# A fp32 transformer block on one core: a chunk's starting sum copied into its PSUM bank during the chunk ahead of it, second-level weights prepared in every second step, four PSUM banks for the projection's last block

## The chip, the core and the metric

The kernel runs on one core of a Trainium2 chip. The metric is the device time of one execution in microseconds (us), read as the median of several runs. TensorE (PE) multiplies, VectorE (DVE), ScalarE (ACT) and GpSimd (POOL) prepare and evacuate, and SyncE (SP) issues every DMA of the kernel in one in-order queue. Each of these engines takes its instructions in the order in which they stand in the program.

## The reference, cut to what matters

```python
def _B_ref(x, w_gate, w_up, w_down):
    return (_gelu(x @ w_gate) * (x @ w_up)) @ w_down
...
h = _layernorm(x, axis=-1) * (1 + ca) + sa
x = x + ga * _A_ref(h, A_wq, A_wk, A_wv, A_wo, A_beta)
h = _layernorm(x, axis=-1) * (1 + cb) + sb
x = x + gb * _B_ref(h, B_w_gate, B_w_up, B_w_down)
```

There are 2048 tokens of width 1024. `_A_ref` is an attention with 32 heads over four segments of 512 tokens, with a running memory from segment to segment, and ends in the output projection `wo`. `_B_ref` is a gated feed-forward block with 3584 hidden columns. All data are fp32; the six rows `sa, ca, ga, sb, cb, gb` come from a small product of `c` and `w_mod`.

## The kernel before

The work on PE is one long list of matmuls, written in the order of the program: opening (modulation and first projections), attention, output projection, feed-forward. An fp32 operand is cut in two parts, a high one (an ACT copy) and a low one (a subtraction on DVE or POOL), and each product is three matmuls: high by high, high by low, low by high. The helper for this is `cut` (ACT line 926, DVE or POOL line 923); in the traces its output carries the name of the tile.

The feed-forward block saves matmuls by forming sums of quarter matrices: `seven` builds seven left operands out of four weight quarters (lines 1079 to 1099), `five` builds five (1101 on). Its stages, in the order in which PE runs them:

- **Projection** (`project`, line 753; called by `block` in `projections`). For each segment and column half it walks over four groups of 128 tokens. A group is 24 matmuls into one bank from `mm_ps`, which has two banks; DVE then adds the bank to a tile of `x` (line 777). The last block is segment 3, half 1. Beside it run generators which prepare the first operands of the next stage (`b_two(0)`, `a_early`, `a_first`).
- **Pairs** (`two`, line 1121), 14 of them. A pair n multiplies seven weight tiles `BB` with seven activation tiles `AA`, for two sets i of activation tiles, in the order r = 1, 5, 6, 2, 7, 3, 4, with i = 1 and then i = 2 for each r (the first pair has all of i = 1 first). A product is six matmuls. They land in the banks `pa`, `pb`, `pc`; `pb` starts from an ACT copy of `pa`, and `ended` evacuates a bank after each product (ACT lines 1156, 1158, 1164; DVE lines 1160, 1162, 1166). The results go to DRAM as `st_d`, one half of them through a gelu (line 1175). The weights of pair n + 1 are built meanwhile by `b_two(n + 1)`. The tiles `BB` live in eight buffers, so each new one takes the buffer of a tile of pair n, and has to wait until PE has used it.
- **Beside the pairs**, from pair 1 on, the generator `norm_tiles(..., "c", wait=6)` normalises the last segment. For each 128 tokens it has PE transpose two halves (`turn`, line 269, banks `tpc` from `o_ps`, which has a single bank); the first half is read by ACT (line 277) and the second by DVE (line 275). The branch of `norm_steps` for `wait` sets how many steps lie between the two (lines 293 to 310). `a_mix(0)` follows it.
- **Chunks** (`gate_up`, line 1359), 56 of them: 28 over the first half of the tokens, and 28 over the second in reverse order. A chunk loads two tiles `cg` from `st_d` (`cg_load`), the sum c1 from which it starts and the gelu g1. It takes two of the five banks `s_ps`: `pb`, into which ACT copies c1 (line 1386), and `pc`. Then come five products of twelve matmuls, in the order 6, 5, 7, 3, 4: 6, 7 and 4 into `pb`, 5 and 3 into `pc`, with evacuations behind each (ACT 1388, 1391; DVE 1394, 1397, 1398) and a last gelu out of `pb` (ACT 1401). In the trace both banks are named `f`.
- **Beside the chunks**, in the first half `b_part(m + 1)` builds the five weight tiles `B` of the next chunk and stores them (`bc_d`, `bt_d`) for the second half, where `b_ahead` and `b_again` load them again seven and six products ahead of their use; a tile `ag`, which `b_again` loads, is cut four products after the load is issued. `a_mix(1)` runs beside chunks 1 to 9. In the second half `w_all` builds the sums of the down weights (POOL multiplies `rw` and forms differences, ACT and DVE cut them as `T`, SP stores them as `wc_d`).
- **Down** (`down`), the last product, with tiles `y`.

What is written beside the matmuls is set by `step()` (line 799): each call sends the stores that are due and advances every generator in the list `sides` by the number of yields that stands with it. A pair calls `step()` after each of its 14 products; a chunk calls it twice in each product, ten times in all. `flush` runs the rest of a generator at once. So the order on ACT, DVE, POOL and SP is the order in which these calls emit.

## Time and profile before

| | us |
|---|---|
| median of 3 runs | 2819.65 (2818.3 to 2819.79) |
| the profiled execution, its own time | 2816.52 |
| its span, first to last instruction | 2814.8 |
| around the span | 1.72 |
| opening and attention end, projection begins | about 910 |
| first pair begins | 1119.72 |
| first chunk begins | 1430.88 |
| down begins | 2277 |

The profile gives for each engine the busy time; a matmul's record is longer than its share of the pipeline, so a busy PE overlaps itself. A row of the timeline has the start, the length, the engine, the line, the operation with its tiles and the count, and in brackets the idle time of the engine ahead of it with what ended it. A row of the windows has, for each engine, the busy time and the number of instructions, then the granted TensorE clock (1.00 is full), the mean busy share of the core's 16 DMA engines and the bytes they moved in GB/s.

### The profile page before, as it was taken

What the parts mean: (1) busy time and instruction counts of PE and PEld (TensorE: products, weight loads), DVE (VectorE), ACT (ScalarE), POOL (GpSimd) and SP (SyncE); (2) the same over time, 40 slices, a digit from 0 to 9 for tenths busy, and PEclk for the clock granted to TensorE, in tenths of its full rate; (3) what the DMA queues carried; (4) which work ended last, traced back from release to release, by engine and by line L of the source; (5) the groups of instructions that cost most, each with busy time, mean ns of one, the idle gap of its engine ahead of it and who ended that gap; (6) DMA issues with size and microseconds to landing.
All of it is one profiled execution on the core that took longest, in us unless ns stands there. A gap on an engine that the chain in (4) does not pass through costs nothing.

```text
span 2814.8 us, 42379 instructions
## 1 busy us (share of the span) xinstructions
PE 2691.4 (96%) x14073; PEld 2218.8 (79%) x14073; DVE 1652.6 (59%) x3540; ACT 1384.8 (49%) x3162; POOL 1013.9 (36%) x1554
## 2 busy tenths in 40 slices
PE   7999999999999999999989999999999999999999
PEld 6888888888888787777767777777777788888887
DVE  7677567667767456655565443454554545475456
ACT  6787777776677443655543333343333333233323
POOL 3333334434335431434357766644655400000000
PEclk9999999999999999999999999999999999999999
DMA  7455445444454485556689777789999887786554
GB/s 254 123 159 139 125 126 164 124 125 128 117 147 135 161 291 176 179 167 226 236 288 318 263 243 251 237 289 343 331 335 342 322 292 250 260 308 221 172 201 133
DMA packets 265644, 612.32 MB, mean 218 GB/s; under 512 B 26960, under 2 KB 51536, under 8 KB 265424
## 3 DMA queue, kind: packets, MB, share of 16 engines
q1 hardware_dynamic: 265424, 609.61, 65.1%
q8 instruction: 111, 1.82, 0.3%
q14 instruction: 109, 0.89, 0.1%
HBM read 371.48 MB, written 187.70 MB: 199 GB/s over the span
## 4 chain that ended last, share of the span: by engine, by line
PE 83%; DMA 5%; DVE 5%; ACT 4%; issue 2%; SPq 1%; POOL 1%; ACTq 0%; DVEq 0%; POOLq 0%
PE f L1375 24%; PE y L1575 18%; PE kv L395 9%; PE q L401 6%; PE y L773 4%; PE S L607 3%; PE O L707 3%; PE T L695 3%; PE pb L1139 3%; PE pc L1139 2%; PE pa L1139 2%; PE vT L514 1%; ACT f L1386 1%; PE kT L514 1%; DMA B<-bc_d 1%
## 5 line engine op out<-in xcount | busy, mean ns | idle before, releaser
L1375 PE MATMUL f<-A,B 128*128 128x512 f32 x3360 | 781.0, 392 | 70.7 <-ACT f L1386 70.7
L1375 PEld LDWEIGHTS f<-A,B 128*128 128x128 f32 x3360 | 627.7, 188 | 223.7 <-ACT f L1386 94.4
L1575 PE MATMUL y<-B,L 128*128 128x512 f32 x2352 | 533.6, 389 | 0.2 <-DVE L L923 0.2
L1575 PEld LDWEIGHTS y<-B,L 128*128 128x128 f32 x2352 | 441.4, 188 | 92.3 <-DVE L L923 0.6
L611 ACT ACTIVATE sj<-sj,mm 128x384 f32<-128x384 f32 (+3 forms) x512 | 281.1, 552 | 40.1 <-DVE mm L609 39.6
L698 POOL TENSOR_SCALAR_AFFINE_SELECT pt<-pt 128x128 f32<-128x128 f32 x512 | 166.6, 347 | 330.9 <-ACT pt L697 322.8
L609 DVE CUSTOM_DVE_ANT_0 sj<-S,mask 128x384 f32<-128x384 f32 (+3 forms) x512 | 228.2, 488 | 97.7 <-PE S L607 70.8
L697 ACT ACTIVATE pt<-T 128x256 f32<-128x256 f32 (+3 forms) x512 | 182.3, 444 | 132.3 <-PE T L695 125.4
L926 ACT ACTIVATE L<-X 128x512 fp32r<-128x512 f32 x168 | 105.7, 629 | 256.3 <-PE y L1575 164.7
L923 DVE TENSOR_TENSOR L<-X,L 128x512 fp32r<-128x512 f32 x168 | 115.8, 690 | 144.9 <-ACT L L926 144.9
L386 POOL TENSOR_TENSOR w<-r,w 128x256 fp32r<-128x256 f32 x180 | 133.8, 774 | 141.6 <-ACT w L380 139.1
L395 PE MATMUL kv<-w,hha 128*128 128x256 f32 x896 | 175.2, 286 | 2.3 <-DVE vx L413 2.3
L1289 POOL TENSOR_TENSOR rw<-rw,gbb 128x256 f32<-128x256 f32 x112 | 105.2, 974 | 182.2 <-DMA rw<-wd 174.8
L923 DVE TENSOR_TENSOR B<-t,B 128x512 fp32r<-128x512 f32 x56 | 52.4, 936 | 164.3 <-ACT B L926 164.3
L395 PEld LDWEIGHTS kv<-w,hha 128*128 128x128 f32 x896 | 145.1, 192 | 3.4 <-DVE vx L413 2.5
L1401 ACT ACTIVATE g<-f 128x512 f32<-128x512 f32 x56 | 33.4, 597 | 231.1 <-PE f L1375 231.1
L923 DVE TENSOR_TENSOR B<-ag,B 128x512 fp32r<-128x512 f32 x81 | 71.7, 886 | 122.7 <-ACT B L926 122.7
L1139 PE MATMUL pb<-AA,BB 128*128 128x512 f32 x504 | 129.3, 401 | 13.6 <-DVE y L1160 8.1
L773 PE MATMUL y<-wo,hho 128*128 128x512 f32 x384 | 127.7, 396 | 2.4 <-DVE xr L777 2.4
L1139 PEld LDWEIGHTS pb<-AA,BB 128*128 128x128 f32 x504 | 95.4, 192 | 41.1 <-DVE y L1160 13.8
L395 PE MATMUL kv<-w,hla 128*128 128x256 f32 x448 | 127.3, 284 | 0.0
L1388 ACT ACTIVATE c<-f 128x512 f32<-128x512 f32 x56 | 33.5, 598 | 168.5 <-PE f L1375 168.5
(290 smaller groups left out, 5256.1 us busy)
## 6 DMA issues: line engine op xcount, KB each, us to landing
B<-wc_d SPq DMA_DIRECT2D x112, 512.0 KB, 3.6
cg<-st_d SPq DMA_DIRECT2D x112, 256.0 KB, 6.2
hid_d<-g SPq DMA_DIRECT2D x56, 512.0 KB, 5.3
wc_d<-T SPq DMA_DIRECT2D x56, 512.0 KB, 5.0
X<-hid_d SPq DMA_DIRECT2D x112, 256.0 KB, 4.7
bc_d<-B SPq DMA_DIRECT2D x54, 512.0 KB, 5.7
B<-bc_d SPq DMA_DIRECT2D x54, 512.0 KB, 6.4
wr<-gd_d SPq DMA_DIRECT2D x84, 256.0 KB, 4.1
```

The costliest lines, as they stand in the source:

```text
L386: nc.gpsimd.tensor_sub(w[:, 1, c], r[:, c], f32(w[:, 0, c]))
L395: nc.tensor.matmul(ps, b[:, sl], w[:, a], start=(kt == 0 and a == 0 and b is hi), stop=(kt == KT - 1 and a == 1), **kw)
L401: nc.tensor.matmul(ps, w[:, a], b, start=(kt == 0 and a == 0 and b is hi), stop=(kt == KT - 1 and a == 1), **kw)
L609: nc.vector.tensor_tensor_reduce(out=sj[:, :nv], in0=ps[:, :nv], in1=mask[:, L - nv:], scale=-1.0, scalar=3.4e38, op0=ALU.add, op1=ALU.min ...
L611: nc.scalar.activation(sj[:, :nv], sj[:, :nv], AF.Exp, bias=mm[:, j, i:i + 1], scale=-1.0, accum_out=ll[:, i, j:j + 1])
L697: nc.scalar.activation(pt, ps[:, nn - n:nn], AF.Exp)
L698: nc.gpsimd.affine_select(pt[:, :P], pt[:, :P], pattern=[[1, P]], compare_op=ALU.is_ge, fill=0.0, base=0, channel_multiplier=-1)
L773: nc.tensor.matmul(ps, b[:, i * P:(i + 1) * P], w[:, a, g % 2], start=(g == 0 and a == 0 and b is hi), stop=(g == G - 1 and a == 1))
L923: f(*xs)
L1139: nc.tensor.matmul(ps, w[:, a, at:at + P], A["a", i, r, k][b], start=(r in (1, 5) and k == a == b == 0), stop=(k == 1 and a == 1), skip_gr ...
L1375: nc.tensor.matmul(ps, B[m, i][:, a, kt * P:(kt + 1) * P], A[p, i, kt][b], start=(start and kt == 0 and a == 0 and b == 0), stop=(kt == 3 ...
L1575: nc.tensor.matmul(banks[t], ops[k][:, y, t * P:(t + 1) * P], B[slots[k]][:, x], start=(i not in (2, 4, 3) and j == 0 and x == 0 and y == ...
```

## The change

The diff makes these edits, and adds or removes no instruction on any engine.

1. `start_sum` allocates a chunk's first bank and issues the ACT copy of c1. It is called for chunk m + 1 inside chunk m, behind the DVE addition that follows product 7, and for chunk 0 behind the last product of the last pair. `gate_up` no longer issues the copy at its start.
2. The two `cg` tiles of chunk 0 come from the pool of `c` tiles in place of the buffers of `A` tiles, and are loaded behind products (2, 2) and (2, 3) of the last pair, that is one each.
3. In `seven` the last four weight tiles are put one in every second step; the difference ahead of them is issued one step earlier. For `b_two(1)`, beside the first pair, two yields are taken in each step.
4. `a_next(0)`, which cuts the `A` tiles of the first half of the chunks, is advanced by one yield in each step in place of two; the loads behind its later iterations, those of the weights of chunk 1 among them, move with it.
5. In `norm_steps` with `wait`, a second yield follows each `turn`.
6. In the projection's last block, groups 2 and 3 take a bank of `s_ps` and the bank of `o_ps`.

```diff
--- before.py
+++ after.py
@@ -308,6 +308,7 @@
                 for h in range(2):
                     turn(q, h)
                     yield
+                    yield
             return
         period, at_stat, at_scale, at_turn = (5, 5, 7, 10) if len(toks) > 4 else (4, 6, 8, 13)
         sts = {}
@@ -765,7 +766,7 @@
             xr = ahead.pop()
             if n + 1 < len(todo):
                 load(*todo[n + 1])
-            ps = mm_ps(f"y{s}_{nb}_{i}")
+            ps = (mm_ps if (s, nb) != (NSEG - 1, 1) or i < 2 else (s_ps, o_ps)[i - 2])(f"y{s}_{nb}_{i}")
             for g in range(G):
                 w = ws[g // 2].rearrange("p h (k m) -> p h k m", m=L)
                 hi, lo = oh[s][g]
@@ -1089,14 +1090,11 @@
             yield
             put(6, t2_, nc.vector)
             yield
-            put(2, b21, nc.vector)
             diff(t2_, b21, t2_)
-            yield
-            put(7, b12, nc.vector)
-            yield
-            put(3, b22, nc.vector)
-            yield
-            put(4, t2_, nc.vector)
+            for r, src in ((2, b21), (7, b12), (3, b22), (4, t2_)):
+                yield
+                put(r, src, nc.vector)
+                yield
 
         def five(b11, b12, b21, b22, t1, t2_, put):
 
@@ -1141,6 +1139,8 @@
                                          skip_group_check=True)
                 if n == NJ - 1:
                     done.add(("a", i, r))
+                    if (i, r) == (2, 4):
+                        start_sum(0, cg[0][0])
 
             def ended(i, r):
                 if r == 1:
@@ -1183,10 +1183,9 @@
                 product(i, r)
                 if n == 0 and (i, r) == (1, 4):
                     b_two_load(2)
-                    sides.append([b_two(1), 1, "b"])
-                if n == NJ - 1 and (i, r) == (2, 3):
-                    for q in range(2):
-                        cg_load(q)
+                    sides.append([b_two(1), 2, "b"])
+                if n == NJ - 1 and (i, r) in ((2, 2), (2, 3)):
+                    cg_load(int(r == 3))
                 ended(i, r)
                 step()
 
@@ -1237,7 +1236,7 @@
 
             p, fc = divmod(m, FC)
             k = (FC - 1 - fc if p else fc) * P
-            cg[m] = [a_tile(40 + 2 * (m % 4) + q, f"cg{m}_{q}", F32) for q in range(2)]
+            cg[m] = [a_tile(40 + 2 * (m % 4) + q, f"cg{m}_{q}", F32) if m else c_tile(f"cg{q}") for q in range(2)]
             for q in range(2):
                 nc.sync.dma_start(cg[m][q], st_d[p][k:k + P, q * L:(q + 1) * L])
 
@@ -1356,6 +1355,12 @@
                     cut(t[:, 0], t[:, 1], again[e], nc.vector)
                     again[e] = None
 
+        started = {}
+
+        def start_sum(m, c1):
+            started[m] = s_ps(f"f0_{m}")
+            nc.scalar.activation(started[m], c1, AF.Copy)
+
         def gate_up(m):
 
             p, fc = divmod(m, FC)
@@ -1379,11 +1384,12 @@
                         step()
                 done.add((m, i))
 
-            pb, pc = (s_ps(f"f{q}_{m}") for q in range(2))
+            if m not in started:
+                start_sum(m, c1)
+            pb, pc = started.pop(m), s_ps(f"f1_{m}")
             u2, u3 = (c_tile(f"c{q}_{m}") for q in range(2))
             g = pair_tile(f"g{m}", "g")
             h1, h2_ = (g[:, q] for q in range(2))
-            nc.scalar.activation(pb, c1, AF.Copy)
             product(pb, 6, False)
             nc.scalar.activation(u2, pb, AF.Copy)
             step()
@@ -1392,6 +1398,8 @@
             step()
             product(pb, 7, False)
             nc.vector.tensor_add(u3, pb, u3)
+            if m + 1 < NCH:
+                start_sum(m + 1, cg[m + 1][0])
             step()
             product(pc, 3, False)
             nc.vector.tensor_add(u2, pc, u2)
@@ -1608,7 +1616,7 @@
             if n == NJ - 2:
                 flush("m")
                 following = a_next(0)
-                sides.append([following, 2])
+                sides.append([following, 1])
             if 0 < n < NJ - 2:
                 b_two_load(n + 2)
             elif n == NJ - 2:
```

The first place is ACT around the start of chunk 3. `g` is the last gelu of a chunk (g2 that of chunk 2), `f0` the copy of c1 into the first bank, `c0` and `c1` the first two evacuations, `B3` the high parts of the weights of chunk 3. Before:

```order
L1386 ACTIVATE f0_2_17601<-cg2_0_17364 128x512
L1388 ACTIVATE c0_2_17603<-f0_2_17601 128x512
L1391 ACTIVATE c1_2_17604<-f1_2_17602 128x512
L926 ACTIVATE B3_6_17647<-t1_3_17615 128x512
L926 ACTIVATE B3_5_17656<-t0_3_17614 128x512
L926 ACTIVATE B3_7_17668<-ru3_17472 128x512
L926 ACTIVATE B3_3_17680<-ru3_17472 128x512
L926 ACTIVATE B3_4_17699<-t1_3_17615 128x512
L1401 ACTIVATE g2_17605<-f0_2_17601 128x512
L1386 ACTIVATE f0_3_17719<-cg3_0_17475 128x512
```

And now:

```order
L1394 ACTIVATE c0_2_17604<-f0_2_17550 128x512
L1397 ACTIVATE c1_2_17605<-f1_2_17603 128x512
L927 ACTIVATE B3_6_17647<-t1_3_17615 128x512
L927 ACTIVATE B3_5_17656<-t0_3_17614 128x512
L1362 ACTIVATE f0_3_17667<-cg3_0_17477 128x512
L927 ACTIVATE B3_7_17670<-ru3_17474 128x512
L927 ACTIVATE B3_3_17682<-ru3_17474 128x512
L927 ACTIVATE B3_4_17701<-t1_3_17615 128x512
L1409 ACTIVATE g2_17606<-f0_2_17550 128x512
L1394 ACTIVATE c0_3_17722<-f0_3_17667 128x512
```

The copy for chunk 3 (f0_3) stood behind the gelu of chunk 2 (g2); it now stands three cuts and that gelu ahead, in the middle of chunk 2.

The second place is ACT beside pair 7. `x7` and `y7` are the results of that pair (`x7_0<-pa7_1` an evacuation, `y7_1<-y7_1` a gelu), and `BB8` are the high parts of the weights of pair 8. Before:

```order
L1158 ACTIVATE y7_1_16167<-pb7_2_16138 128x512
L926 ACTIVATE BB8_2_16188<-g8_0_15944 128x512
L1164 ACTIVATE x7_0_16199<-pa7_1_16114 128x512
L926 ACTIVATE BB8_7_16204<-g8_1_15945 128x512
L926 ACTIVATE BB8_3_16216<-g8_1_15945 128x512
L1175 ACTIVATE y7_0_16213<-y7_0_16213 128x512
L926 ACTIVATE BB8_4_16227<-t2_a8_16125 128x512
L1175 ACTIVATE y7_1_16167<-y7_1_16167 128x512
L1164 ACTIVATE x7_0_16199<-pb7_1_16121 128x512
L1175 ACTIVATE y7_1_16167<-y7_1_16167 128x512
```

And now:

```order
L1158 ACTIVATE y7_1_16160<-pb7_2_16134 128x512
L1164 ACTIVATE x7_0_16190<-pa7_1_16110 128x512
L927 ACTIVATE BB8_2_16193<-g8_0_15940 128x512
L1175 ACTIVATE y7_0_16202<-y7_0_16202 128x512
L927 ACTIVATE BB8_7_16213<-g8_1_15941 128x512
L1175 ACTIVATE y7_1_16160<-y7_1_16160 128x512
L927 ACTIVATE BB8_3_16239<-g8_1_15941 128x512
L1164 ACTIVATE x7_0_16190<-pb7_1_16117 128x512
L1175 ACTIVATE y7_1_16160<-y7_1_16160 128x512
L927 ACTIVATE BB8_4_16260<-t2_a8_16121 128x512
```

The four weight tiles stood nearly together, ahead of the gelus of the pair; now each is followed by one or two pieces of the pair's own work. On DVE the low parts have moved in the same way.

The third place is PE beside pair 3, where `tpc1664_0` and `tpc1664_1` are the two transposed halves of 128 tokens. Before, from the end of product (1, 1) to the start of product (1, 5):

```order
L1139 MATMUL pa3_1_15381<-AA1_1_1_0_14329,BB3_1_15223 128x512
L269 MATMUL tpc1664_0_15391<-ident_113,nc1664_15236 128x128 x4
L1139 MATMUL pa3_2_15408<-AA2_1_0_0_14713,BB3_1_15223 128x512
...
L1139 MATMUL pa3_2_15408<-AA2_1_1_0_14731,BB3_1_15223 128x512
L269 MATMUL tpc1664_1_15418<-ident_113,nc1664_15236 128x128 x4
L1139 MATMUL pc3_1_15430<-AA1_5_0_0_14635,BB3_5_15250 128x512
```

And now, behind product (1, 5):

```order
L269 MATMUL tpc1664_0_15419<-ident_113,nc1664_15260 128x128 x4
L1137 MATMUL pc3_2_15432<-AA2_5_0_0_14745,BB3_5_15248 128x512
...
L1137 MATMUL pc3_2_15432<-AA2_5_1_0_14754,BB3_5_15248 128x512
L1137 MATMUL pb3_1_15388<-AA1_6_0_0_14650,BB3_6_15272 128x512
...
L1137 MATMUL pb3_1_15388<-AA1_6_1_0_14662,BB3_6_15272 128x512
L269 MATMUL tpc1664_1_15450<-ident_113,nc1664_15260 128x128 x4
L1137 MATMUL pb3_2_15405<-AA2_6_0_0_14758,BB3_6_15272 128x512
```

One product (`pa3_2`) stood between the two halves; now there are two (`pc3_2` and `pb3_1`), of six matmuls each.

## The prediction

> **What bounds the kernel now.** I read the page first, then what PE waited for, then the stretches in which it waited. The page says that PE is busy nearly all the time; so what can be gained is what PE waits for, and no other engine's busy time counts by itself.
>
> ```profile
> PE 2691.4 (96%) x14073; PEld 2218.8 (79%) x14073; DVE 1652.6 (59%) x3540; ACT 1384.8 (49%) x3162; POOL 1013.9 (36%) x1554
> ```
>
> The list of PE's waits (total us, number of times, the longest) has one large entry, and five more that the change touches:
>
> ```profile
> PE f L1375 <- ACT f L1386: 70.7, 56, 5.8
> PE pb L1139 <- DVE y L1160: 8.1, 12, 0.9
> PE tpc L269 <- ACT htc L277: 7.0, 4, 2.4
> PE pb L1139 <- DVE x L1160: 5.4, 4, 2.9
> PE y L773 <- DVE xr L777: 2.4, 2, 1.5
> PE pa L1139 <- DVE xr L777: 1.9, 1, 1.9
> ```
>
> Every chunk starts with a wait for the copy on line 1386. The timeline shows the reason:
>
> ```profile
> 1476.69 0.60 ACT L1401 ACTIVATE g<-f 128x512 f32<-128x512 f32 x1 [2.50 <-PE f L1375]
> 1477.18 0.60 ACT L1386 ACTIVATE f<-cg 128x512 f32<-128x512 f32 x1
> 1477.83 13.89 PE L1375 MATMUL f<-A,B 128*128 128x512 f32 x60 [1.18 <-ACT f L1386]
> 1483.61 0.60 ACT L1391 ACTIVATE c<-f 128x512 f32<-128x512 f32 x1 [2.12 <-PE f L1375]
> 1484.10 1.15 ACT L926 ACTIVATE B<-t 128x512 fp32r<-128x512 f32 x2
> 1485.14 1.14 ACT L926 ACTIVATE B<-ru 128x512 fp32r<-128x512 f32 x2
> ```
>
> The copy needs nothing of the chunk before, but it stands on ACT behind that chunk's gelu (line 1401), and the gelu needs PE's last matmul. So PE drains, two ACT instructions of 0.60 us run, and PE starts again.
>
> A wait's idle time understates its cost, since a matmul's record overlaps the next one's. The honest price is the pace of matmuls without waits, which the chain shows in the last stage, and the pitch of the chunks by the first and last start of the copy:
>
> ```profile
> 2294.16 516.88 PE y L1575 x2279
> L1386 ACT ACTIVATE f<-cg x56: 582/597/597, 1430.2 to 2262.8; 128x512 f32<-128x512 f32 x56
> ```
>
> A matmul takes 516.88 / 2279 = 0.2268 us there, so 60 of them 13.61 us. The 55 pitches between the 56 copies take 2262.8 - 1430.2 = 832.6 us, 15.14 each. Without waits they would take 55 x 13.61 = 748.6. The difference, **84.0 us**, is what the first edit can bring inside the chunks.
>
> **The change part by part.** No engine gets more or fewer instructions, and no transfer is added: the price of the change is only in order.
>
> *The copy ahead (edit 1).* It now stands on ACT behind the two cuts that follow line 1391, that is at about 1485.2 in the timeline above, 6 us before the chunk's end. Its bank, one of five, was last read two chunks earlier, and c1 was loaded more than a chunk earlier, so nothing holds it there. The 0.60 us that it takes in the middle delays three cuts for the next chunk, and behind them ACT waits for PE at the gelu (2.50 us above), which covers it. If all goes so, the 84.0 us go. What is late next is the supply: everything beside a chunk must now be done in 13.61 us in place of 15.1.
>
> ```profile
> 1430.90:1853.00 422.10, 390.23 (x1675) 313.74 (x1676) 191.64 (x219) 145.07 (x263) 277.09 (x318) 1.00 0.78 263
> 1853.00:2277.00 424.00, 390.96 (x1690) 314.74 (x1690) 217.73 (x265) 140.78 (x259) 207.54 (x224) 1.00 0.91 326
> 1871.50:2233.20 361.70, 333.48 (x1440) 268.46 (x1440) 188.20 (x221) 119.53 (x220) 203.41 (x220) 1.00 0.93 335
> 2142.80:2157.80 15.00, 13.89 (x60) 11.18 (x60) 6.08 (x9) 3.77 (x8) 4.72 (x6) 1.00 1.02 390
> 2294.00:2811.00 517.00, 516.85 (x2279) 427.66 (x2279) 289.07 (x450) 164.26 (x274) 0.00 (x0) 1.00 0.66 227
> ```
>
> These windows are the first 28 chunks, the last 28, the 24 chunks of these in which the transfers are thickest, the thickest single chunk, and the down stage. The columns behind the length are PE, its weight loads, DVE, ACT, POOL, then the granted clock, the DMA share and GB/s. POOL, the busiest helper, is at 277.09 / 422.10 = 66% in the first half and would be at 73%: enough room. The transfers are the question. The 24 chunks move 335 GB/s; at a pitch of 13.61 they must move 335 x 361.7 / (24 x 13.61) = 371 GB/s, and their share of 0.93 would become 1.03. One chunk has shown 390 GB/s at a share of 1.02 with PE undisturbed (13.89 busy of 15.00, as in any chunk). So the demand lies at the edge of what the rows show. Bounds: nothing lost, or the share held at 1.00, which makes these chunks last 361.7 x 0.93 = 336.4 us and not 326.6: 9.8 lost. I take 4, nearer to the row at 390, which is above 371. The Trainium skill, in "DMA: Bandwidth & Descriptors", section "Where 436 GB/s comes from", puts the limit of one core between HBM and SBUF at about 358 GB/s: by it (an estimate) the 24 chunks would last 361.7 x 335 / 358 = 338.5 us, 11.9 lost. With that rule the trace's row at 390 GB/s over a whole chunk disagrees. The clock is no danger by the rows: PE ran 516.85 of 517.00 us at 1.00.
>
> Another us goes in chunk 0: the last eight cuts of `A`, which stood in the last pair, now stand in it ahead of the products that need them (bounds 0 and 3 us, a product being 12 x 0.2268 = 2.72). Edit 1 and 2 thus give **84.0 - 4 - 1 = 79**.
>
> *The end of the last pair (edits 1, 2 and 4).*
>
> ```profile
> 1417.00:1424.00 7.00, 3.94 (x11) 2.44 (x10) 6.97 (x11) 3.46 (x7) 1.68 (x3) 0.79 0.97 343
> 1424.00:1431.00 7.00, 1.19 (x5) 0.64 (x3) 6.24 (x8) 3.22 (x7) 4.93 (x5) 0.74 0.83 306
> ```
>
> DVE is full here (6.97 of 7.00) with cuts of `A`, and PE waits for it: 2.9 us (the longest wait for line 1160 as x) and then 5.8 (the longest for line 1386). With the clock, (1 - 0.79) x 3.94 + (1 - 0.74) x 1.19 = 1.1, that is 9.8. Eight of the `A` cuts now lie behind this place, and the copy no longer waits for the tail. ACT still has an evacuation, a gelu, a cut and the copy behind product (1, 4), 2.4 us against the 6 x 0.2268 = 1.36 of the last product: I keep 1.5 of waiting and take **8.3** (bounds 4 and 9.8).
>
> *Weights in every second step (edit 3).*
>
> ```profile
> 1255.81 1.52 PE L1139 MATMUL pb<-AA,BB 128*128 128x512 f32 x6
> 1256.07 0.63 ACT L926 ACTIVATE BB<-t_a 128x512 fp32r<-128x512 f32 x1 [1.62 <-PE pc L1139]
> 1256.74 0.69 DVE L923 TENSOR_TENSOR BB<-t_a,BB 128x512 fp32r<-128x512 f32 x1 [1.25 <-ACT BB L926]
> 1257.35 0.68 DVE L1160 TENSOR_TENSOR y<-pb,y 128x512 f32<-128x512 f32 x1
> 1258.08 1.65 PE L1139 MATMUL pb<-AA,BB 128*128 128x512 f32 x6 [0.75 <-DVE y L1160]
> 1259.57 2.90 PE L1139 MATMUL pa<-AA,BB 128*128 128x512 f32 x12
> 1279.67 2.90 PE L1139 MATMUL pa<-AA,BB 128*128 128x512 f32 x12
> ```
>
> The cut of the last weight tile stands too early: ACT waits in it for a buffer that PE is just using (`pc`), DVE waits for ACT, and the evacuation of `pb` behind both comes 0.75 us late for the pair's last product. The pitch of such a pair is 1279.67 - 1259.57 = 20.10 us; 84 matmuls take 19.05. So it costs 1.05 in each of 11 pairs (the twelfth wait is in the last pair, above), 11.6. In the new order each cut comes a product after its buffer was freed, and DVE's evacuation stands ahead of it. I keep 1 and take **10.6** (bounds 6 and 11.6).
>
> *A second yield behind each `turn` (edit 5).*
>
> ```profile
> 1212.10 1.63 PE L1139 MATMUL pc<-AA,BB 128*128 128x512 f32 x6
> 1216.13 1.08 PE L269 MATMUL tpc<-ident,nc 128*128 128x128 f32 x4 [2.40 <-ACT htc L277]
> 1214.00:1221.00 7.00, 4.87 (x17) 4.01 (x18) 2.65 (x6) 3.68 (x9) 0.00 (x0) 0.76 1.00 323
> 1242.00:1249.00 7.00, 6.19 (x22) 5.05 (x23) 2.66 (x6) 4.00 (x9) 1.16 (x2) 0.76 0.57 198
> ```
>
> The second half waits until ACT has emptied the single bank; two of the four waits also drop the clock to 0.76 for a window, 0.24 x (4.87 + 6.19) = 2.7 us. With the 7.0 of the list that is 9.7. Another product of 1.36 us between the halves takes at most 4 x 1.36 = 5.4 of the waits, and leaves too little idle time for the clock to fall. I take **7.2** (bounds 4 and 9.7).
>
> *Four banks (edit 6).*
>
> ```profile
> 1116.00:1123.00 7.00, 5.13 (x19) 3.76 (x18) 5.40 (x9) 2.85 (x6) 0.00 (x0) 0.83 0.23 87
> 1123.00:1130.00 7.00, 6.79 (x28) 5.26 (x26) 5.58 (x7) 4.77 (x10) 1.88 (x2) 0.92 0.01 4
> ```
>
> The waits for line 777 (2.4 and 1.9) go, since each group has a bank of its own. The clock behind them is worth 0.17 x 5.13 + 0.08 x 6.79 = 1.4, and three waits for line 1160 in the pairs another 2.5. But DVE is late here in any case: what it still has to cut comes no sooner, and PE meets it a little further on. Of these 8.2 I take **3.5** (bounds 0 and 8.2).
>
> *What else moves, at no cost.* The later `turn`s push `a_mix(0)` back by eight steps, 8 x 1.36 = 11 us; what it stores is loaded in pair 12 and first cut in pair 13, a pair of 19 us later, and if that cover failed, the price would be SP standing in the load, with the pairs' stores behind it, which nobody on PE waits for. On SP the loads of chunk 1's weights now stand behind most of the last pair's stores; POOL needs them for tiles that PE takes a chunk, 13.61 us, later, and if they land late, chunk 0's 3 us above are the price. The slower `b_two(0)` delays `a_early` by a few steps in the projection, two blocks ahead of its use.
>
> The sum is 79 + 8.3 + 10.6 + 7.2 + 3.5 = **108.6 us**. The profiled execution took 2816.52, so 2707.9 in its terms; the median is 3.1 above it, which gives **2711**.
>
> **The rivals.** *The second half of the chunks is bound by the transfers.* The share stays at 1.00 and the loss there is 9.8, not 4: 2711 + 5.8 = **2717**. For it speaks the share of 0.93, against it the row at 390. Chance 0.20. By the rule of the Trainium skill above the loss would be 11.9, and the time 2719.
>
> *The stalls of the pairs form again.* DVE and ACT have as much to do as before, and PE waits for the next thing in their queues; the last four terms (29.6) bring 5: **2736**. For it speaks DVE's 6.97 of 7.00 at the end, against it DVE's 2.65 and 2.66 of 7.00 at the transposes. Chance 0.08.
>
> *The copy does not come early.* In the second half it stands behind cuts of `T`, for which POOL must have its product, and POOL waits for loads. If ACT reaches it only at the chunk's end, half of the 79 stays: **2751**. Against it: in the second half ACT is busy 140.78 of 424.00 us. Chance 0.08.
>
> *Slower.* The copy and two evacuations now all stand on ACT behind cuts that read loaded tiles. If the loads fall behind by more than their lead, ACT stands in each chunk.
>
> ```profile
> ag<-bt_d SPq DMA_DIRECT2D x48, 256.0 KB, 5.4
> ```
>
> This landing time of 5.4 us (the median of the 24 chunks) compares with a lead of four products, 10.9 us. At twice the landing time ACT begins to wait; if it then waits one landing in each of the last 27 chunks, 27 x 5.4 = 146 us are lost, 108.6 are won, and the time is **2857**. It decides from 108.6 / 27 = 4.0 us per chunk on. The row at 390 GB/s, with PE undisturbed, speaks against it. Chance 0.03.
>
> **How the numbers follow.** The forecast keeps 0.61. The best ends of all bounds give 84.0 + 9.8 + 11.6 + 9.7 + 8.2 = 123.3, or 2696; the poor ends 84.0 - 9.8 - 3 + 4 + 6 + 4 + 0 = 85.2, or 2734, and with the second rival's 2736 and some us for what I do not see, 2742. So the range is 2695 to 2742. It leaves out the last two rivals and some of the forecast's tail. A change within 0.2% (5.6 us, what a measurement of this kernel can tell from none) needs a loss of about 105 in the chunks: 0.01. Slower 0.03, faster 0.96.
>
> **What would show it.** The wait for the copy's line should be gone from PE's list or be below 5 us, the copies should start about 13.7 us apart in both halves, and PE's list should hold neither `y L1160` nor `xr L777` above 2 us. The windows of the last 28 chunks should show about 360 GB/s at a share near 1; a wait of ACT's `B` or `T` cuts for DMA or POOL there would be the first rival or the third. The forecast is wrong if the pitch of the first 28 chunks, where no transfer limits, stays above 14.2 us, or if PE waits elsewhere in a chunk for ACT or DVE.

## The result, and the profile after

The changed kernel takes 2712.57 us (median of 4 runs, 2709.86 to 2713.46), the kernel before beside it 2818.98 (4 runs, 2814.51 to 2819.79). The ratio is 0.9624, with a 95% interval of 0.9607 to 0.9641. The profiled execution took 2709.86 us with a span of 2708.1, against 2816.52 and 2814.8: 106.7 us less, where the forecast's sum had 108.6.

The page's busy times are what they were, and PE's share rises to 99%:

```profile
PE 2669.0 (99%) x14073; PEld 2224.1 (82%) x14073; DVE 1652.2 (61%) x3540; ACT 1383.8 (51%) x3162; POOL 1008.2 (37%) x1554
```

The list of PE's waits (total us, number of times, the longest) has lost its large entry. The copy (now line 1362) is waited for once, not 56 times. Two larger waits ahead of these lines, 11.1 and 3.8 us, belong to the opening, which no edit touches:

```profile
...
PE f L1380 <- ACT f L1362: 3.5, 1, 3.5
PE pb L1137 <- DVE x L1160: 3.4, 1, 3.4
PE f L1380 <- ACT A L927: 2.9, 1, 2.9
...
PE tpc L269 <- ACT htc L277: 1.3, 2, 1.1
```

The entry for `xr` is gone, and `y L1160` has 0.2 us left. The timeline of PE (start, length, and behind the number of matmuls the idle time ahead of them) shows the chunks as three long blocks with two gaps at the start, where each chunk had been a row of its own:

```profile
1398.45 13.91 PE L1380 MATMUL f<-A,B 128*128 128x512 f32 x48 [3.46 <-ACT f L1362]
1415.30 311.84 PE L1380 MATMUL f<-A,B 128*128 128x512 f32 x1362 [2.94 <-ACT A L927]
...
1729.69 441.22 PE L1380 MATMUL f<-A,B 128*128 128x512 f32 x1944
```

The last block has 441.22 / 1944 = 0.2270 us a matmul, which is the pace without waits of the forecast (0.2268), over 32 chunks. A table by stage says where the time came from. Each stage is read from the timeline of PE in the profiled execution: it begins at the stage's first matmul and ends where the next one begins (down: at the end of its last matmul).

| stage | before, us | after, us | saved |
|---|---|---|---|
| opening and attention | 908.4 | 908.2 | 0.2 |
| projection | 211.3 | 206.7 | 4.6 |
| pairs, and the way into chunk 0 | 311.2 | 283.5 | 27.6 |
| 56 chunks | 846.3 | 772.3 | 74.0 |
| down | 533.8 | 533.6 | 0.2 |

Of the chunks' ideal 56 x 13.61 = 762.1 us, 10.2 are still missing, and most of them lie in chunk 0. These are windows of 4 us around its start, with the granted clock, as the mean of the window, behind the five busy times:

```profile
1394.00:1398.00 4.00, 0.99 (x5) 0.49 (x3) 3.33 (x7) 2.91 (x7) 0.00 (x0) 0.94 1.06 381
1398.00:1402.00 4.00, 3.54 (x8) 2.84 (x9) 2.53 (x4) 2.10 (x4) 0.00 (x0) 0.50 1.00 392
1402.00:1406.00 4.00, 4.00 (x14) 3.20 (x13) 0.87 (x2) 1.64 (x3) 0.00 (x0) 0.71 1.04 404
1406.00:1410.00 4.00, 4.00 (x20) 3.30 (x19) 1.12 (x2) 1.12 (x2) 1.61 (x2) 1.00 1.03 394
...
1414.00:1418.00 4.00, 2.70 (x7) 2.15 (x7) 4.00 (x6) 2.27 (x5) 4.00 (x5) 0.57 0.32 131
1418.00:1422.00 4.00, 4.00 (x12) 3.15 (x11) 3.55 (x5) 0.75 (x2) 4.00 (x5) 0.58 0.72 183
```

PE waits 3.46 us for chunk 0's copy, and the two windows of 4 us behind have a mean clock of 0.50 and 0.71; it waits 2.94 us for a cut of `A`, and the next two have 0.57 and 0.58. The missing share of the clock times the busy time is 0.50 x 3.54 + 0.29 x 4.00 = 2.93 us behind the first wait and 0.43 x 2.70 + 0.42 x 4.00 = 2.84 behind the second, 5.8 together. With the wait of 2.94 that is 8.7 of the 10.2. The reasons for the waits stand on ACT and POOL:

```profile
1396.77 0.63 ACT L1175 ACTIVATE y<-y 128x512 f32<-128x512 f32 x1 [1.09 <-DVE y L1162]
1397.30 0.61 ACT L927 ACTIVATE A<-ra 128x512 fp32r<-128x512 f32 x1
1397.82 0.58 ACT L1362 ACTIVATE f<-cg 128x512 f32<-128x512 f32 x1
...
1411.53 0.63 ACT L927 ACTIVATE B<-t 128x512 fp32r<-128x512 f32 x1 [3.44 <-POOL t L924]
```

The copy stands behind a gelu (line 1175) that waits for DVE. The cut of `A` stands behind a cut of `B`, for which ACT waits until POOL has made its difference, and POOL has waited 17.59 us for chunk 1's weights, whose load was issued only at 1401.26.

Last, the transfers. The first window is the last 28 chunks, the second the 24 in which they are thickest:

```profile
1790.00:2170.80 380.80, 380.80 (x1682) 315.32 (x1681) 215.69 (x261) 139.82 (x256) 207.46 (x224) 1.00 0.98 362
1799.00:2125.00 326.00, 326.00 (x1440) 269.93 (x1439) 187.46 (x221) 120.04 (x220) 202.41 (x218) 1.00 1.00 370
```

The 370 GB/s that the forecast worked out are moved, and PE has no idle time beside them.

### The profile page after: what moved, and what is told of

Its sections match the earlier page's. It is cut to its first block, busy times and chain, and to the rows that moved or that the text cites. A ratio compares the mean times of both kernels' runs of the same rounds, so it can differ in the third digit from the quotient of the medians.

```text
span 2708.1 us, 42385 instructions
## 1 busy us (share of the span) xinstructions
PE 2669.0 (99%) x14073; PEld 2224.1 (82%) x14073; DVE 1652.2 (61%) x3540; ACT 1383.8 (51%) x3162; POOL 1008.2 (37%) x1554
## 4 chain that ended last, share of the span: by engine, by line
PE 55%; DMA 1%; DVE 1%; ACT 1%; issue 0%; POOL 0%; SPq 0%; ACTq 0%; POOLq 0%
PE f L1380 28%; PE y L1583 20%; PE pb L1137 3%; PE pa L1137 2%; PE pc L1137 2%; DMA cg<-st_d 0%; DMA ru<-wu 0%; DMA mix_d<-rm 0%; DVE y L1162 0%; DVE BB L924 0%; ACT BB L927 0%; DVE y L1160 0%; ACT y L1175 0%; POOL t L924 0%; PE tpc L269 0%
## 5 line engine op out<-in xcount | busy, mean ns | idle before, releaser
L1380 PE MATMUL f<-A,B 128*128 128x512 f32 x3360 | 768.9, 391 | 6.4 <-ACT f L1362 3.5
L1380 PEld LDWEIGHTS f<-A,B 128*128 128x128 f32 x3360 | 634.6, 189 | 140.4 <-ACT f L1362 3.9
L1583 PE MATMUL y<-B,L 128*128 128x512 f32 x2352 | 533.6, 389 | 0.0
L924 DVE TENSOR_TENSOR B<-t,B 128x512 fp32r<-128x512 f32 x56 | 53.0, 947 | 120.1 <-ACT B L927 120.1
L696 PE MATMUL T<-qs,ks 128*128 128x256 f32 (+3 forms) x512 | 105.6, 327 | 1.7 <-DVE ry L675 1.1
```

Source lines behind the costliest of these rows:

```text
L924: f(*xs)
L1380: nc.tensor.matmul(ps, B[m, i][:, a, kt * P:(kt + 1) * P], A[p, i, kt][b], start=(start and kt == 0 and a == 0 and b == 0), stop=(kt == 3 ...
L1583: nc.tensor.matmul(banks[t], ops[k][:, y, t * P:(t + 1) * P], B[slots[k]][:, x], start=(i not in (2, 4, 3) and j == 0 and x == 0 and y == ...
```

## The experiments

My theory after the result: the chunks' gain is the copy's place and nothing else; the pairs' gain is edits 3 and 5; edits 4 and 6 move waits without removing them; and the transfers have room left. The rivals stand with each run. Edit 2 was not undone by itself. Line numbers shift by a few lines from kernel to kernel. Times are medians, and each ratio is to runs of the kernel before beside them; the stages are those of the table above, with the time at which the projection begins ahead of them.

| kernel | median, us | ratio to before, 95% interval | projection begins | projection | pairs | chunks |
|---|---|---|---|---|---|---|
| after | 2712.57 | 0.9624 (0.9607 to 0.9641) | 908.2 | 206.7 | 283.5 | 772.3 |
| no_early_copy | 2792.39 | 0.9917 (0.9901 to 0.9932) | 906.9 | 206.7 | 283.3 | 850.9 |
| copy_alone | 2733.65 | 0.9710 (0.9694 to 0.9726) | 909.7 | 211.4 | 307.7 | 765.8 |
| weights_every_step | 2725.71 | 0.9681 (0.9667 to 0.9695) | 910.8 | 206.4 | 297.8 | 773.1 |
| one_yield | 2726.31 | 0.9685 (0.9670 to 0.9699) | 911.0 | 206.8 | 297.6 | 771.9 |
| two_banks | 2711.69 | 0.9630 (0.9616 to 0.9645) | 912.3 | 211.0 | 279.1 | 770.2 |
| a_cuts_two | 2712.68 | 0.9635 (0.9620 to 0.9649) | 907.2 | 206.8 | 289.3 | 766.4 |
| more_1 | 2710.15 | 0.9629 (0.9613 to 0.9645) | 910.0 | 206.7 | 282.4 | 771.2 |
| more_2 | 2740.38 | 0.9734 (0.9720 to 0.9747) | 910.9 | 206.8 | 283.1 | 802.3 |
| more_4 | 2805.51 | 0.9962 (0.9948 to 0.9976) | 910.9 | 206.7 | 283.8 | 864.5 |
| entry_early | 2705.63 | 0.9607 (0.9593 to 0.9622) | 909.5 | 206.8 | 279.9 | 770.2 |
| entry_late_b | 2709.65 | 0.9621 (0.9607 to 0.9634) | 909.7 | 206.7 | 280.1 | 771.7 |
| entry_all | 2701.82 | 0.9598 (0.9585 to 0.9611) | 907.0 | 206.8 | 279.7 | 764.3 |

The projection lasts 206.4 to 206.8 us in the eleven kernels with four banks. What differs is when it begins, 906.9 to 912.3 us, behind an opening and an attention that no edit touches. So a difference of the totals below 5 us says little; the stage that an edit touches says more.

**The copy, taken back and alone.** no_early_copy:

```diff
             nc.vector.tensor_add(u3, pb, u3)
-            if m + 1 < NCH:
-                start_sum(m + 1, cg[m + 1][0])
...
-                    if (i, r) == (2, 4):
-                        start_sum(0, cg[0][0])
```

> The changed kernel with the copy back at each chunk's start; edits 2 to 6 stay. Theory (the copy's place is what the chunks gained, 74.0 us from the first chunk to the down stage, 846.3 before and 772.3 after): the chunks take 846 us again, PE's list has the wait for the copy 56 times with about 70 us, the pitch is 15.1 us, and the time is about 2712.6 + 74 = 2787 us (2780 to 2792). Rival (the chunks gained by the work beside them, spread by edits 2 to 5): the chunks stay below 800 us, and the time below 2740.

copy_alone, from the kernel before:

```diff
+            if m not in started:
+                start_sum(m, c1)
+            pb, pc = started.pop(m), s_ps(f"f1_{m}")
...
-            nc.scalar.activation(pb, c1, AF.Copy)
...
             nc.vector.tensor_add(u3, pb, u3)
+            if m + 1 < NCH:
+                start_sum(m + 1, cg[m + 1][0])
```

> The kernel before with the early copy alone, for chunks 1 to 55. Theory (the edits add up, each in its own stretch): the pairs take 311 us as before, the chunks gain 70 to 76 us, and the time is about 2819.0 - 74 = 2745 us (2740 to 2752). Rival (with the cuts of the old order in chunk 0 and the weights as they were, the supply can't follow the shorter pitch): the chunks gain less than 50 us, and the time is above 2765.

Without the early copy, PE's waits and its timeline have the old pattern again:

```profile
PE f L1378 <- ACT f L1360: 68.8, 56, 4.0
```

```profile
1568.88 13.90 PE L1378 MATMUL f<-A,B 128*128 128x512 f32 x60 [1.18 <-ACT f L1360]
1583.95 13.90 PE L1378 MATMUL f<-A,B 128*128 128x512 f32 x60 [1.18 <-ACT f L1360]
```

The pitch is 15.07 us, the chunks take 850.9, and the pairs 283.3 as in the changed kernel. The copy alone, in the kernel before, makes the chunks dense (timeline of PE):

```profile
1428.87 322.14 PE L1381 MATMUL f<-A,B 128*128 128x512 f32 x1410 [4.83 <-ACT f L1363]
1751.30 1.96 PE L1381 MATMUL f<-A,B 128*128 128x512 f32 x6
1753.56 441.22 PE L1381 MATMUL f<-A,B 128*128 128x512 f32 x1944
```

The chunks take 765.8 us. The copy's place is worth 850.9 - 772.3 = 78.6 us taken back and 846.3 - 765.8 = 80.6 alone, and needs no other edit. Both totals moved by more than I had expected (79.8 and, from its own before of 2816.16, 82.5): the first lies just above its range, the second 6 us below. The rival, that the other edits feed the shorter pitch, falls: this kernel's chunk 0, with the cuts of `A` still in the pair, is even without the 2.94 us wait.

**The pairs' two edits.** weights_every_step and one_yield:

```diff
-            for r, src in ((2, b21), (7, b12), (3, b22), (4, t2_)):
-                yield
-                put(r, src, nc.vector)
-                yield
+            put(2, b21, nc.vector)
+            yield
+            put(7, b12, nc.vector)
+            yield
+            put(3, b22, nc.vector)
+            yield
+            put(4, t2_, nc.vector)
...
-                    sides.append([b_two(1), 2, "b"])
+                    sides.append([b_two(1), 1, "b"])
```

> The changed kernel with the last four weight tiles of a pair put in four steps in a row again (edit 3 undone). Theory (the stall of 1.05 us a pair came from the cut that stands ahead of the evacuation): y L1160 returns to PE's list with 11 or 12 waits and about 8 us, the pitch of the pairs is 20.1 us in place of 19.04, and the time rises by 10 to 12 us, to about 2723. Rival (the stall went with the other edits' order on DVE and ACT): the pitch stays below 19.4 us and the time rises by less than 4 us.

```diff
                     turn(q, h)
                     yield
-                    yield
```

> The changed kernel with one step between the two halves of a transpose (edit 5 undone). Theory: four waits of tpc for htc come back, 7 us together in place of 1.3, the granted clock falls to about 0.76 for a window behind two of them, worth another 2.7 us, and the time rises by 7 to 9 us, to about 2720. Rival (the waits return but the clock does not fall, or PE catches up in the pair): the time rises by 3 to 6 us.

The weights in consecutive steps bring the stall back, once in a pair. First PE's wait, then two starts of a pair in the timeline:

```profile
PE pb L1140 <- DVE y L1163: 8.1, 12, 1.0
```

```profile
1251.66 2.88 PE L1140 MATMUL pa<-AA,BB 128*128 128x512 f32 x12
1271.74 2.88 PE L1140 MATMUL pa<-AA,BB 128*128 128x512 f32 x12
```

The pitch is 20.08 us again, against 19.04 in the changed kernel, and the pairs take 14.3 us more: 12 x 1.04 = 12.5 for these waits, and 1.5 for the transposes' waits, which grow as well (1.9 and 0.9 against 1.3). I had expected 10 to 12. With one step between the halves, the transposes wait longer than they did before the change (7.0 us then), and the windows of two pairs show the clock:

```profile
PE tpc L269 <- ACT htc L277: 11.6, 4, 3.9
```

```profile
1172.00:1210.00 38.00, 34.35 (x149) 28.04 (x148) 21.62 (x39) 18.33 (x33) 12.85 (x17) 0.96 0.45 155
1210.00:1248.00 38.00, 31.32 (x138) 24.97 (x137) 19.32 (x35) 22.43 (x42) 8.86 (x11) 0.96 0.52 172
```

The waits grow by 11.6 - 1.3 = 10.3 us and the clock costs 0.04 x (34.35 + 31.32) = 2.6, together 12.9 of the 14.1 us that the pairs lose. My expectation of 7 to 9 was too low. My reading is that PE, without the stalls of edit 3, comes to the transpose earlier, and ACT empties the bank no sooner: what one edit saves, the other stall takes. So edit 5 is worth more once edit 3 is done. No run has one of the two alone in the kernel before, so this is not shown beyond the 7.0 and 11.6 us.

**Two edits that move a wait.** two_banks and a_cuts_two:

```diff
-            ps = (mm_ps if (s, nb) != (NSEG - 1, 1) or i < 2 else (s_ps, o_ps)[i - 2])(f"y{s}_{nb}_{i}")
+            ps = mm_ps(f"y{s}_{nb}_{i}")
```

> The changed kernel with two banks for the projection's last block (edit 6 undone). Theory (DVE is late there in any case, so a bank only moves where PE meets it): the waits for xr L777 return with about 4 us, the stretch from the projection's start to the first pair grows by 2 to 5 us (115.2 now), the first pair's wait for x L1160 shrinks from 3.4 to below 2 us, and the time rises by 1 to 4 us, to about 2715. Rival (the four waits and the clock behind them were the whole loss, 8.2 us): the time rises by 6 to 9 us.

```diff
-                sides.append([following, 1])
+                sides.append([following, 2])
```

> The changed kernel with the next pass's cuts of A at two per step again (edit 4 undone). Theory (edit 4 only moves DVE's burst of cuts from the last pair into chunk 0): the pairs last 5 to 8 us longer than 283.5, the chunks 4 to 7 us less than 772.3, and the time changes by 0 to 3 us, to about 2714. Rival (the forecast's term for the end of the last pair, 8.3 us, belongs to these cuts and chunk 0 gains little): the time rises by 6 to 8 us, to about 2720.

With two banks PE waits for `xr` again, and less for the first pair's evacuation:

```profile
PE pb L1137 <- DVE x L1160: 1.9, 1, 1.9
PE pa L1137 <- DVE xr L778: 1.9, 1, 1.9
PE y L774 <- DVE xr L778: 1.7, 2, 1.6
```

The first pair's window shows the other side, first for two banks and then for the changed kernel:

```profile
1115.00:1134.00 19.00, 15.25 (x66) 11.95 (x65) 17.12 (x25) 9.21 (x17) 4.13 (x6) 1.00 0.35 120
```

```profile
1115.00:1134.00 19.00, 14.61 (x56) 11.03 (x55) 14.71 (x22) 10.34 (x19) 7.69 (x10) 0.91 0.40 135
```

With four banks the projection takes 206.7 us (mean of 11 kernels) and not 211.3 (mean of 3 with two banks, the kernel before among them). The 115.2 us that I named ahead of the run count from 999.7 us, in the middle of the projection; from its first matmul two_banks is 4.3 us longer than the changed kernel, within what I expected. Of the 4.6 us the pairs give back 4.1 (279.1 against 283.2, the mean of the five kernels with the changed kernel's pairs, itself among them): the first pair waits longer for DVE, and the clock falls to 0.91. The total differs by less than a measurement can tell, where I had expected a rise of 1 to 4 us without the two further banks.

With the cuts at two per step PE waits 6.1 us for DVE at `x L1160` in place of 3.4, and 4.7 for the copy in place of 3.5:

```profile
PE pb L1137 <- DVE x L1160: 6.1, 2, 3.3
PE f L1380 <- ACT f L1362: 4.7, 1, 4.7
```

The pairs take 5.8 us more and the chunks 5.9 less. Edit 4 moved DVE's burst from the last pair into chunk 0, and that is all: the two differences cancel to 0.1 us.

**How far the transfers carry.** more_1, more_2 and more_4 add transfers that nothing uses to the chunks of the second half. more_1 (more_2 does it for both loads of a chunk):

```diff
...
                     src, k = bc_d, (NCH - 1 - e[0]) * 2 + WHOLE.index(e[1])
+                    for c in range(2 if e[1] == 6 else 0):
+                        spare.append(a_tile(52 + len(spare) % 4, f"ex{len(spare)}", F32))
+                        nc.sync.dma_start(spare[-1], src[k * P:(k + 1) * P, c * L:(c + 1) * L])
```

> The changed kernel with a transfer added: in each chunk of the second half two loads of 256 KB into tiles that nothing reads, 38 GB/s on top of the 370 that its 24 thickest chunks move at a share of 1.00. Theory of a ceiling just above (375 to 390 GB/s): 408 GB/s are asked for, these chunks last 5 to 9% longer, and the time rises by 15 to 30 us, to 2728 to 2743. Rival 1 (a limit of 358 GB/s, already reached by bursts only): 14%, about 45 us, to 2758. Rival 2 (a share of 1.00 is no ceiling): below 3 us.

> As more_1 with twice the addition: in each chunk of the second half four loads of 256 KB that nothing reads, 77 GB/s, so that the 24 thick chunks ask for 447 GB/s. Theory (410 GB/s went by with PE undisturbed and the loads landing in 7.6 us, under the lead of 10.9 us; a ceiling lies further on): the stretch still takes its 13.61 us a chunk, the landing times grow to 8 to 10 us, and the time changes by less than 4 us, to 2708 to 2717. Rival (the ceiling is at about 415 GB/s, just above the addition of more_1): 24 chunks last 447 / 415 as long, and the time rises by about 25 us, to 2738.

more_4, on top of more_2:

```diff
...
+                        if e[0] > FC + 2:
+                            kept = A[1, e[1], c][0]
+                            nc.sync.dma_start(sp_d[len(spare) * P:(len(spare) + 1) * P], f32(kept))
```

> As more_2 with four stores of 256 KB a chunk beside the four loads, from tiles of A that are kept, into a scratch tensor: 154 GB/s, so that the thick chunks ask for 524 GB/s. Theory (somewhere the transfers must limit, and the share of 1.04 at 410 GB/s says that it is not far): the stretch moves 430 to 470 GB/s, 12 to 20% longer than its 327 us, PE waits for the cuts of B behind their loads, and the time rises by 35 to 70 us, to 2748 to 2783. Rival (no limit that this kernel can meet): 524 GB/s are moved and the time rises by less than 5 us.

The same window as above (share and GB/s stand last), for more_1, more_2 and more_4:

```profile
1799.00:2125.00 326.00, 326.00 (x1440) 269.95 (x1439) 178.47 (x220) 120.52 (x220) 191.93 (x215) 1.00 1.03 407
```

```profile
1799.00:2125.00 326.00, 310.77 (x1340) 250.43 (x1338) 148.96 (x201) 111.89 (x203) 156.02 (x192) 0.99 1.03 405
```

```profile
1799.00:2125.00 326.00, 285.68 (x1166) 226.26 (x1164) 124.96 (x175) 96.94 (x175) 134.91 (x171) 0.95 1.04 404
```

407 GB/s pass with PE busy for all of the 326 us. Asked for 447 or 524, the transfers give 405 and 404: there is the ceiling of this kernel, at a share of 1.03 to 1.04. The time follows from it: 24 x 13.61 x 447 / 405 = 360.5 us for the thick chunks of more_2, 33.9 more, where its chunks took 802.3 - 772.3 = 30.0 more. For more_4 the same sum gives 97 us, measured 92.2. So for more_1 I expected a ceiling at 375 to 390 GB/s, and that fell; for more_2 the rival was right, and for more_4 I expected 430 to 470 GB/s and a rise of 35 to 70 us, where 404 and 92.9 were measured. The overload is seen on SP, not in the landing times (between 1880 and 2100 us, 7.2 us for the loads of `B` in the changed kernel, 7.6 in more_1, 7.4 in more_2). These are SP's three largest waits in more_2 in the window of 326 us, and ACT's largest:

```profile
SPq L1344 <- DMA B<-bc_d: 21.5, 24, 1.8
SPq L1339 <- DMA ex<-bc_d: 14.3, 49, 0.3
SPq L1307 <- DMA wc_d<-T: 11.2, 13, 1.0
```

```profile
ACT B L927 <- DMA ag<-bt_d: 141.6, 37, 6.5
```

SP stands before an issue until an earlier transfer is done, and everything behind it in the queue is late: ACT stands in the cuts of the `ag` tiles until these land, which in the changed kernel it does not. There SP waits for DVE instead (120.1 us for the results that it stores), so its queue is ahead of the work. The issue and landing times of the traces show what SP waits for: in none of the 14 kernels is a transfer issued before the one eight issues earlier has landed, so at most eight are under way. In more_2, 329 of the 354 issues of the window come within 0.1 us of that landing. So these runs do not show whether the ceiling is that of the transfers' engines or that of eight transfers at a time.

**The way into chunk 0.** The last three runs look for the 10.2 + 3.5 us that the changed kernel leaves there. entry_early:

```diff
-                    if (i, r) == (2, 4):
+                    if (i, r) == (2, 3):
                         start_sum(0, cg[0][0])
...
-                if p == 0 and q == 6:
+                if p == 0 and q == 4:
                     gu_load(1)
```

> The changed kernel with two things earlier in the last pair: chunk 0's copy behind product (2, 3) in place of (2, 4), and the loads of chunk 1's weights two cuts of A earlier. Theory (PE's 3.46 us at chunk 0 are the copy behind a gelu on ACT, its 2.94 us a cut of A behind a cut of B for which POOL waits for those loads): both waits fall below 1 us, the granted clock stays near 1.00 in chunk 0, and the time falls by 6 to 9 us, to about 2705. Rival (SP stands in the earlier loads until their buffers are free, or DVE's cuts of A are what is late): one wait goes and another comes, and the time falls by less than 3 us.

```profile
1396.11 11.51 PE L1380 MATMUL f<-A,B 128*128 128x512 f32 x48 [0.24 <-ACT f L1362]
1411.06 2.53 PE L1380 MATMUL f<-A,B 128*128 128x512 f32 x10 [3.45 <-ACT A L927]
```

Half of the theory held. The copy's wait fell from 3.46 to 0.24 us, and the 48 matmuls behind it take 11.51 us and not 13.91. The loads were issued 6 us earlier, but POOL got the second one only at 1404.03, and the cut of `A` still waits 3.45; a new wait of 1.73 us for DVE came at the start of chunk 1. The median fell by 6.9 us, within what I expected, but the intervals of the two ratios overlap; by the stages it is 3.6 in the pairs and 2.1 in the chunks.

The clock is not explained by the waits alone. Behind the 3.45 us that stay in entry_early it is 1.00 in each window of 4 us from 1402 to 1418, where the changed kernel has 0.57 and 0.58 behind 2.94 us. And in one_yield PE waits for the copy as long as in the changed kernel, and the 48 matmuls behind take 11.17 us and not 13.91:

```profile
1415.36 11.17 PE L1379 MATMUL f<-A,B 128*128 128x512 f32 x48 [3.47 <-ACT f L1361]
```

So the 5.8 us of slow clock in the changed kernel's chunk 0 do not follow from the length of its two waits, and part of what entry_early gains in the chunks may be luck.

entry_late_b, on top of it, and entry_all, on top of that:

```diff
-                sides.append([b_part(m + 1), 1, "b"])
+                sides.append([chain(wait_for(0 if m else 3), b_part(m + 1)), 1, "b"])
```

> entry_early with the preparation of chunk 1's weights begun three steps later, so that chunk 0's last cuts of A stand ahead of the first cut of B on ACT. Theory (the 3.4 us left in chunk 0 are ACT standing in a cut of B whose difference POOL makes from a load landed at 1404): that wait goes, the clock stays at 1.00 in chunk 0, and the time falls by another 3 to 5 us, from 2705.6 to about 2702. Rival (the weights are then late for chunk 1): PE waits at the start of chunk 1 for a cut of B by about as much, and the time stays at 2704 to 2708.

```diff
-                for _ in range(4):
+                for _ in range(4 if kt or not p else 8):
                     yield
                 a11, a21, a12, a22 = r[0][:, :h], r[0][:, h:], r[1][:, :h], r[1][:, h:]
```

> entry_late_b with four more steps between the first loads of the second pass's mixes (in chunk 1) and DVE's first use of them. Theory (the 6.1 us that PE waits there in chunk 1 are DVE standing in that use, with the evacuation for PE behind it, until the load has landed): the wait goes, chunks 0 and 1 run without a gap, the chunks take 765 to 767 us in place of 771.7, and the time falls from 2709.7 to about 2703. Rival (the load is late by more than 5.4 us, or the cuts of B behind it are what is late): a wait of 2 us or more stays in chunk 1 and the time stays above 2706.

With the weights' preparation three steps later chunk 0 runs through without a gap, but the time, 2709.65, is 4.0 above entry_early's (the chunks 1.5, and the intervals overlap): a longer wait came in chunk 1, not the one that my rival named. DVE and PE in entry_late_b:

```profile
1426.13 0.97 DVE L961 TENSOR_TENSOR m<-rm,rm 128x512 f32<-128x512 f32 x1 [4.94 <-DMA rm<-h_d]
1427.02 0.68 DVE L1400 TENSOR_TENSOR c<-f,c 128x512 f32<-128x512 f32 x1
```

```profile
1427.76 17.58 PE L1380 MATMUL f<-A,B 128*128 128x512 f32 x70 [6.12 <-DVE c L1400]
```

DVE stands 4.94 us in the first sum of the second pass's mixes, whose load was issued at 1417.40, and the evacuation that PE needs stands behind it. The gap in chunk 0 had hidden most of that load's lateness: entry_early waits 1.73 us at the same place. Four more steps ahead of the sum remove this wait as well. PE in entry_all:

```profile
1393.43 25.08 PE L1380 MATMUL f<-A,B 128*128 128x512 f32 x108 [0.22 <-ACT f L1362]
1418.74 295.42 PE L1380 MATMUL f<-A,B 128*128 128x512 f32 x1302 [0.23 <-DVE c L1400]
```

The chunks take 764.3 us, 2.2 above the ideal, and the time is 2701.82 us, a ratio of 0.9598 (0.9585 to 0.9611). This version beats both kernels by its median. Its interval touches that of the changed kernel, but pairs and chunks together take 1044.0 us against 1055.8, and they are where the edits are.

## Why the prediction was right, and where its terms were not

The forecast, 2711 us, lies 1.6 below the measured median, and the mechanism of the main term is shown by no_early_copy and copy_alone. The copy is waited for once (3.5 us, below the 5 that I had named), and the chunks of the first half have a pitch of (1726.98 - 1415.30) / 1362 x 60 = 13.73 us by the timeline, where 14.2 would have spoken against me. But the sum came out so well because errors of both signs met. And one sign that I had named against the forecast did appear, once: PE waits elsewhere in a chunk for ACT, 2.94 us in chunk 0, and in none of the other 55.

- **The copy ahead (79 forecast).** The chunks saved 74.0. The 84.0 us of the working were nearly right: copy_alone, without the burden in chunk 0, saved 80.6. The 4 us for the transfers were not lost; the bound "the share held at 1.00" is not one, since the share goes to 1.04 and the rate to 407 GB/s. The 1 us for chunk 0 was mis-sized: it was 2.94 of waiting and 5.8 of slow clock. The wait is the one that the prediction named, chunk 1's weights landing late, and at its upper bound of 3; the clock was not in the sum. The step that failed there is "The clock is no danger by the rows", which I took from the down stage, where nothing waits; the rows of the transposes, with 0.76 behind a wait of 2.4 us, were the nearer ones. Even these do not settle it: behind waits of 3.5 us the clock stayed at 1.00 in one_yield and entry_early.
- **The end of the last pair (8.3 forecast).** Mis-sized. Of the wait for the copy 3.46 us stayed where I kept 1.5: I had counted ACT's work behind product (1, 4), but not that a gelu in it waits for DVE. And what edit 4 gains in the pairs, 5.8 us, chunk 0 pays back with 5.9 (a_cuts_two).
- **Weights in every second step (10.6 forecast).** Undone, it costs 14.3 us in the pairs. The mechanism and the price of 1.05 us a pair are right. I kept 1 for safety and counted eleven pairs; the wait comes back twelve times (12.5), and the transposes wait 1.5 longer.
- **The second yield (7.2 forecast).** Undone, it costs 14.1. I priced it by the waits before the change, 7.0 us, which are 11.6 once the other stall is gone. My upper bound of 9.7 was too low for that reason.
- **Four banks (3.5 forecast).** Nothing that can be measured: 4.6 us are gained ahead of the pairs, and 4.1 are given back in the first pair. The sentence that PE meets DVE "a little further on" was right, and should have been carried to its end.

The two terms of the pairs were about 10 us too low by these runs (17.8 forecast, 28.4 undone), and the other three too high: the chunks by 5, the last pair by up to 8, the banks by about 3. Undone runs don't add up exactly, since a stall that one edit removes makes another's longer.

The rivals: *bound by the transfers* (2717) is refuted for this kernel by more_1, which moves 37 GB/s more at no cost in time. The Trainium skill, "DMA: Bandwidth & Descriptors", section "Where 436 GB/s comes from", puts the limit of one core at about 358 GB/s, half of a memory stack's 716; the runs, with one core at work, show 407 over 326 us. *The stalls of the pairs form again* (2736) did not happen for the two large ones, but it is what happened to edits 4 and 6. *The copy does not come early* (2751) did not happen: no chunk after the first waits for it. *Slower* (2857) needs a demand that the transfers cannot follow. Its mechanism, ACT standing in cuts of tiles not yet loaded, shows in more_2 and more_4; but even 524 GB/s asked for cost 93 us, less than the change brings, and the changed kernel's own demand of 370 does not come near.

What stays open: why the projection begins up to 5 us earlier or later behind the same work, what besides the length of a wait makes the clock fall, and whether the ceiling of about 405 GB/s stays with more than eight transfers under way.

## What to carry to other kernels

When an instruction needs nothing of the work just finished but stands behind it in an engine's queue, count a drain of the matrix engine for each pass, and move the instruction one product ahead: here 1.4 us in each of 56 chunks, by one line. An edit that only moves work off a crowded place should be followed to where the work arrives: with DVE or a load late in any case, PE waits for the same thing a little later. Price a wait of PE of some 3 us with and without a slow clock behind it, and take the bound of a transfer rate from a run that overloads it, not from the busy share.

## What the runs showed of the hardware

A single gap can cost more than its length, and its length alone does not say whether it does. In the changed kernel the granted clock behind the waits of 3.46 and 2.94 us was 0.50 to 0.71 over two windows of 4 us each. Behind 3.47 us in one_yield and 3.45 us in entry_early it stayed at 1.00, as it did behind the waits of 1.18 us at each chunk of the kernel before. The Trainium skill, "TensorE: Matmul & The Clock Gate", section "HAM oscillation — how this bites in real kernels", has the rule that a pause of PE above about 3.4 us makes its clock drop. The traces do not bear it out as a rule on the length of a wait in the profile: 2.94 us were enough in one kernel, and 3.47 were not in another. And the busy share of the transfers is no measure of what is left: more_1 moved a tenth more than the 370 GB/s that went with a share of 1.00. When the rate stood still at 405 GB/s the landing times did not grow, since SP had no more than eight transfers under way: the issuing queue stood instead.
